# Attention with two expert layers: ACT's and DVE's copies out of the same PSUM banks modelled as taking turns, and the whole order made anew

## The chip, the cores and the metric

One core of a Trainium2 chip runs the program. The metric is the device time of one execution in microseconds (us). PE is the matrix engine, PEld its loading of weights, DVE the vector engine, ACT the scalar engine, POOL the GpSimd engine, SP the engine that issues the transfers.

## What is computed

Three stages follow each other: an attention in which a query sees only the keys whose 6 sign bits agree with its own, a layer with x·tanh(softplus(x)), and a layer with softmax times x and a layer norm. Inputs: q, k, v of 2 batches x 8 heads x 768 tokens x 64, `proj` 64 x 6, weights 512 x 2048 and back, 512 x 1024 and back (float64, read as pairs of 32-bit words).

```python
def _attn_ref(q, k, v, proj) -> np.ndarray:
...
    q_bits = (np.einsum('bhsd,dk->bhsk', q, proj) > 0).astype(np.int64)
    k_bits = (np.einsum('bhsd,dk->bhsk', k, proj) > 0).astype(np.int64)
...
    mask = q_bucket[:, :, :, None] == k_bucket[:, :, None, :]
    scores = scale * np.matmul(q, k.transpose(0, 1, 3, 2))
    scores = np.where(mask, scores, -1000000000.0)
...
    return np.matmul(attn, v).astype(np.float32)
...
def _moe_ref(x, w_in, w_out) -> np.ndarray:
    h = x @ w_in
    sp = np.where(h > 20.0, h, np.log1p(np.exp(np.minimum(h, 20.0))))
    g = h * np.tanh(sp)
    return (g @ w_out).astype(np.float32)
...
def _moe2_ref(x, w_in, w_out, g_ln) -> np.ndarray:
    h = x @ w_in
...
    solu = h * sm
...
    return (ln @ w_out).astype(np.float32)
```

## The kernel before, in words

**The stages.** The 16 heads are worked on in 8 pairs (0 to 7). Each head has 6 tiles of 128 queries by 768 keys, so there are 96 tiles. A tile's steps are `score` (PE, L1238), `max` (DVE, L1245) and `bias` (DVE, two one-column rows, L1249 and L1250), `exp` (ACT, L1254), a split of the result into two f16 halves and its transposition (by DMA for four tiles in six; for the two others by PE, L1273, ACT, L1277, and DVE, `tlo`, L1282), and `weigh`, the product with v (PE, L1305 to L1307). The first expert layer has 48 units, each of 12 products up, 11 element steps (`mi`) on ACT, DVE and POOL, and 12 products down. The second has 12 tiles. Weights come as 48 chunks (`w`): a load, a first step on ACT (L728), four on DVE (L730, L732, L734, L736), one on ACT and one on POOL or DVE. Eight chunks (0 to 7) are meant for the time of the attention, the others for that of the first layer.

**The preparation of a pair.** While the tiles of pair n-1 run, pair n is prepared. For each of its two heads and for q and k, PE makes 6 transposes into two PSUM banks (`turn`, L1163), and ACT copies the banks out into a tile A (`evac`, L1180, 128 partitions). For q a second copy of half of the same banks goes to a tile B on DVE (L1171, 64 partitions). There are 16 of these second copies, two for each pair. For k the rest of B comes by DMA (`copy`). PE then multiplies A with the projection (`bits`, L1204), DVE compares (`sign`, L1212), and small DMAs put the bits into B. Only then can the pair's scores start. `vmax` (DVE, L1091) and some one-column steps `vs` prepare v.

**What sets the order.** A scheduler in the program, class `Order`, sets the order of all instructions on all engines before they are issued. It knows a cost for each step (`COST`), a delay from engine to engine (`LATENCY`) and the rings and banks. Of the steps that could start within 0.1 us of the earliest it takes the one that is due first. A step's due time is its place in the work plus an offset of its kind from `PHASE`, some 130 numbers. Nothing moves at run time: each engine works its list from top to bottom, and where a step waits, all behind it on that engine wait too. In the scheduler's model before, the first and second copies of the same banks (`("evac", n, h, 0)` and `("evac", n, h, 2)`) are two readers that may run at the same time:

```python
op(("evac", n, h, o), A if e == "A" else V, COST["evac" + e], d, "evac" + f, [s], [("A%d" % o, n, h)])
if again and (o if n == 0 else not o):
    g = again[h]
    op(("evac", n, h, 2), A if g == "A" else V, COST["evac" + g], d, "evac" + f, [("st", n, h, 0)],
       [("B", n, h, 0)])
```

Of the kernel before, what the change touches and what calls it, by code (L numbers as in the profile page):

```python
# [32 lines left out]
    score=2.89, max=21.69, bias=-20.48, exp=-7.37, hi=37.60, lo=-74.88, tdma=47.79, tr0=9.51, thi0=14.05,  # L33
    tlo0=2.17, tr1=10.84, thi1=28.04, tlo1=16.57, weigh=17.46, norm0=29.45, norm1=6.67, norm2=-77.92,
    load=19.06, vload=18.96, split0=-188.88, rest0=28.62, split1=-216.02, rest1=37.27, turn=-44.19,
    evac=-204.06, copy=-27.06, bits0=-103.88, bits1=-136.11, sign=51.37, bdma=40.93, vmax=21.86, vs0=-271.50,
    vs1=9.08, vs2=-210.73, vs3=-129.45, vs4=-56.64, vs5=-127.12, vs6=-290.81, vs7=144.62, vs8=-328.13,
    vh=70.16, vl=45.25, first=63.48, turn_=6.48, evac_=195.41, copy_=-35.91, bits_=94.54, sign_=168.35,
    bdma_=-9.06, vload_=-304.47, vmax_=171.56, vs_=87.04, vh_=-22.87, vl_=-122.68, second=35.58, wload=28.78,
    w0=-41.17, w1=84.02, w2=-26.10, w3=26.15, w4=31.29, w5=19.05, w6=290.37, wpace=-25.50, wat=214.24,  # L40
    wlate=-420.19, turngap=-246.21, x0_=-6.98, x1_=-173.02, x2_=44.49, load_=10.81, const0=66.52,
    begin0=-146.26, vs8_=150.21, outlag=-5.17, up=-162.02, a0=-14.23, a1=40.52, a2=25.54, a3=14.48, a4=30.07,
    a5=-71.43, a6=11.38, a7=-135.40, a8=-17.97, a9=76.71, a10=229.81, da=51.52, db=-112.61, ky0=101.10,
    ky1=110.82, x0=37.16, x1=118.52, x2=72.93, sy0=21.03, sy1=8.66, u2=24.00, n0=-198.44, n1=78.28, n2=130.92,
    n3=-69.22, n4=-178.31, n5=-31.52, n6=140.09, n7=224.60, n8=-279.51, n9=-111.63, n10=-196.61, n11=-61.38,
    n12=-275.68, n13=3.09, t2=-8.41, l0=-92.90, l1=222.42, d2=202.96, ot=-141.26, od=-47.76, wloadL=-156.21,
    w0L=2.89, w1L=23.01, w2L=229.21, w3L=-26.73, w4L=229.00, w5L=-89.36, w6L=-69.41, begin1=-117.25,
    begin2=-102.32, begin3=76.98, const1=123.70, const3=67.06, load0_=-1.00,
)


# [25 lines left out]
class Order:  # L77
# [38 lines left out]
    def shared(self, o):  # L116
# [7 lines left out]
        if k in ("hi", "sy", "mg"):  # L124
            return True
# [12 lines left out]
    def run(self):  # L138
# [64 lines left out]
        for _ in range(n):  # L203
            best = None
            for e, line in queue.items():
                cand = []
                for r, i in line:
                    r = max(r, free[e])
                    if ops[i][7]:
                        r = ring(i, r)[0]  # L210
                        if r is None:
                            continue
# [1203 lines left out]
```

## Time and profile before

| what | us |
|---|---|
| three timed runs: median, lowest, highest | 654.56, 653.5, 655.46 |
| profiled execution, its own time | 653.04 |
| span of its trace, first to last instruction | 651.3 |

The profiled execution took 1.7 us more than its span, for what lies before the first and after the last instruction. In rows of the trace, times count from the span's start, a row gives start and duration in us, engine, line, operation, what is written and read, and in brackets how long the engine had been idle before it and what ended that.

### The profile page before, as it was taken

How to read it: one execution, taken by the hardware profiler on the slowest of the kernel's cores; microseconds unless marked ns; L12 is line 12 of the kernel's file. 1: busy time of each engine (PE TensorE's matmuls, PEld its weight loads, DVE VectorE, ACT ScalarE, POOL GpSimd, SP SyncE). 2: the span in 40 equal slices, each digit the busy share in tenths (PEclk: the TensorE clock that was granted, in tenths of full speed). 3: DMA queues.
4: the chain of work that ended last, by engine and by line, in shares of the span. 5: the costliest groups of instructions: out<-in, count | busy, mean ns of one | idle time of the engine just before them, and what ended most of it. 6: DMA issues, size and time to landing. Idle time of an engine off the chain costs nothing.

```text
span 651.3 us, 12308 instructions
## 1 busy us (share of the span) xinstructions
PE 622.2 (96%) x4460; PEld 513.1 (79%) x4460; DVE 558.7 (86%) x1149; ACT 444.0 (68%) x722; POOL 367.5 (56%) x301
## 2 busy tenths in 40 slices
PE   7889999999899899999999999999999999999997
PEld 6668787888778788878888777788788888788885
DVE  4899798898989999999999999999999776675652
ACT  5689897998999986766565566656566545565543
POOL 4678868777765675566666666455476421222210
PEclk9799899999999999999999999999999999999999
DMA  7979978989898892312333322212121022322221
GB/s 203 219 166 148 243 162 159 170 212 166 180 186 165 151 205 76 97 50 79 98 98 97 98 97 66 94 61 70 35 97 34 1 64 45 81 71 81 66 64 49
DMA packets 146909, 73.36 MB, mean 113 GB/s; under 512 B 125344, under 2 KB 139808, under 8 KB 146848
## 3 DMA queue, kind: packets, MB, share of 16 engines
q1 hardware_dynamic: 146848, 72.58, 47.5%
q8 instruction: 35, 0.57, 0.4%
q14 instruction: 26, 0.21, 0.1%
HBM read 34.68 MB, written 3.15 MB: 58 GB/s over the span
## 4 chain that ended last, share of the span: by engine, by line
PE 42%; DVE 22%; ACT 6%; issue 5%; DMA 1%; POOL 0%; DVEq 0%; ACTq 0%; SPq 0%
PE banks L835 4%; PE banks L837 3%; PE banks L940 3%; PE banks L836 3%; PE banks L944 3%; PE banks L941 3%; PE banks L896 3%; PE banks L891 3%; PE banks L892 3%; PE banks L1029 3%; PE banks L1027 3%; DVE mx L1245 3%; PE banks L1028 3%; DVE a L865 2%; DVE a L853 2%
## 5 line engine op out<-in xcount | busy, mean ns | idle before, releaser
L1287 POOL TENSOR_TENSOR store<-store 128x768 f16<-128x768 f32 x64 | 104.9, 1651 | 48.6 <-ACT store L1265 44.3
L1254 ACT ACTIVATE store<-banks,mx 128x768 f32<-128x768 f32 x96 | 92.4, 998 | 12.3 <-DVE mx L1250 5.0
L1245 DVE TENSOR_REDUCE mx<-banks 128x1 f32<-128x768 f32 x96 | 89.4, 946 | 3.1 <-PE banks L1238 2.0
L869 POOL TENSOR_TENSOR n<-c,a 128x512 f32<-128x512 f32 x48 | 63.8, 1329 | 44.6 <-DVE a L865 42.3
L877 POOL TENSOR_TENSOR gl<-n,gh 128x512 fp32r<-128x512 f32 x48 | 62.9, 1310 | 33.4 <-ACT gh L874 33.0
L835 PE MATMUL banks<-xh,w 128*128 128x512 f32 x192 | 76.6, 399 | 2.5 <-DVE a L865 1.6
L891 PE MATMUL banks<-gh,w 128*128 128x512 f32 x192 | 75.8, 395 | 0.9 <-ACT gh L874 0.8
L837 PE MATMUL banks<-xh,w 128*128 128x512 f32 x192 | 75.7, 394 | 0.0
L836 PE MATMUL banks<-xl,w 128*128 128x512 f32 x192 | 75.4, 393 | 0.0
L892 PE MATMUL banks<-gh,w 128*128 128x512 f32 x192 | 75.3, 392 | 0.0
L859 ACT ACTIVATE a<-n,two 128x512 f32<-128x512 f32 x48 | 34.8, 724 | 56.7 <-DVE n L855 56.4
L896 PE MATMUL banks<-gl,w 128*128 128x512 f32 x192 | 72.4, 394 | 0.0
L743 POOL TENSOR_TENSOR w<-wf,w 128x512 fp32r<-128x512 f32 x40 | 51.7, 1293 | 35.2 <-ACT w L741 33.9
L1238 PE MATMUL banks<-A,A 128*128 128x384 f32 x192 | 58.5, 387 | 8.4 <-ACT store L1254 7.4
L1305 PE MATMUL banks<-v,store 128*128 128x65 f16 x576 | 60.0, 193 | 2.3 <-DVE store L1282 1.9
L1306 PE MATMUL banks<-v,store 128*128 128x64 f16 x576 | 59.8, 194 | 0.0
L1307 PE MATMUL banks<-v,store 128*128 128x65 f16 x576 | 59.6, 192 | 0.0
L1305 PEld LDWEIGHTS <-store 128*128 128x128 f16 x576 | 53.0, 96 | 5.0 <-issue 4.6
L1306 PEld LDWEIGHTS <-store 128*128 128x128 f16 x576 | 53.3, 97 | 2.9 <-issue 2.5
L1265 ACT ACTIVATE store<-store 128x768 f16<-128x768 f32 x64 | 53.3, 849 | 0.2
L1307 PEld LDWEIGHTS <-store 128*128 128x128 f16 x576 | 53.5, 99 | 0.0
L1238 PE MATMUL banks<-B 76*128 76x384 f32 x192 | 51.5, 350 | 0.0
(131 smaller groups left out, 1731.7 us busy)
## 6 DMA issues: line engine op xcount, KB each, us to landing
wr<-in_moe_w_in_dram SPq DMA_DIRECT2D x24, 512.0 KB
wr<-in_moe_w_out_dram SPq DMA_DIRECT2D x24, 512.0 KB
vr<-in_v_dram SPq DMA_DIRECT2D x8, 384.0 KB
B<-A SPq DMA_DIRECT2D x16, 192.0 KB
out_dram<-ot SPq DMA_DIRECT2D x12, 256.0 KB
q<-in_q_dram SPq DMA_DIRECT2D x7, 384.0 KB
k<-in_k_dram SPq DMA_DIRECT2D x7, 384.0 KB
B<-bits SPq DMA_DIRECT2D x32, 36.0 KB
```

The costliest lines, as they stand in the source:

```text
L835: nc.tensor.matmul(h, lhsT=wh[:, ks], rhs=xh, start=(kk == 0), stop=False)
L836: nc.tensor.matmul(h, lhsT=wh[:, ks], rhs=xl, start=False, stop=False)
L837: nc.tensor.matmul(h, lhsT=wl[:, ks], rhs=xh, start=False, stop=(kk == KD - 1))
L891: nc.tensor.matmul(y, lhsT=wh[:, os], rhs=g_t[u][0], start=first, stop=False)
L892: nc.tensor.matmul(y, lhsT=wl[:, os], rhs=g_t[u][0], start=False, stop=False)
L1238: nc.tensor.matmul(s[:, half, 0:NH], lhsT=opnd[nm, p, j, 0][:, cc], rhs=opnd[nm, p, j, 1][:, hs], start=(i == 0), stop=(i == 1),)
L1245: nc.vector.reduce_max(m[:, 1:2], two_banks("s", t)[:, :, 0:NH], axis=AX.XY, negate=True)
L1254: nc.scalar.activation(kept("e", t).rearrange("p (a n) -> p a n", a=2), two_banks("s", t)[:, :, 0:NH], AF.Exp, bias=m[:, 3:4], scale=m[:, ...
L1287: nc.gpsimd.tensor_tensor(p16[:, 1], kept("e", t), p16[:, 0], op=ALU.subtract)
L1305: nc.tensor.matmul(o, lhsT=pt[:, 0, kc, :], rhs=vh, start=(kc == 0), stop=False)
L1306: nc.tensor.matmul(o[:, 0:D], lhsT=pt[:, 0, kc, :], rhs=vl, start=False, stop=False)
L1307: nc.tensor.matmul(o, lhsT=pt[:, 1, kc, :], rhs=vh, start=False, stop=(kc == NC - 1))
```

## The change

The scheduler gets a rule: of the ACT copy to A and the DVE copy to B of the same banks, whichever is put second becomes ready only when the first is done, plus the delay between the engines. All numbers of `PHASE` were set anew, and with them the order of all instructions on all engines is another one. The same instructions are issued, as many of each kind and size. Two more ways of making the second copy, from tile A, on ACT (`a`) or on DVE (`v`), are written into the code; `again` is still "VV", so they are not used.

```diff
 PHASE = dict(
-    score=2.89, max=21.69, bias=-20.48, exp=-7.37, hi=37.60, lo=-74.88, tdma=47.79, tr0=9.51, thi0=14.05,
+    score=3.38, max=19.53, bias=-65.87, exp=-8.79, hi=46.12, lo=-15.66, tdma=47.09, tr0=9.55, thi0=-33.26,
...
@@ -82,6 +83,7 @@
         self.spare = dict(e=2, p16=1)
+        self.other, self.port = {}, set()
...
@@ -210,6 +212,9 @@
                         if r is None:
                             continue
+                    k = self.other.get(i)
+                    if k is not None and done[k] is not None:
+                        r = max(r, done[k] + LATENCY[frm[k]].get(e, 0.0))
                     cand.append((r, due[i], i))
...
@@ -326,8 +331,13 @@
                     g = again[h]
-                    op(("evac", n, h, 2), A if g == "A" else V, COST["evac" + g], d, "evac" + f, [("st", n, h, 0)],
-                       [("B", n, h, 0)])
+                    op(("evac", n, h, 2), A if g in "Aa" else V, COST["evac" + g], d, "evac" + f,
+                       [("st", n, h, 0) if g in "AV" else ("A0", n, h)], [("B", n, h, 0)])
+                    if g == "v":
+                        order.port.add(("evac", n, h, 2))
+                if again and (o if n == 0 else not o) and g in "AV":
+                    a, b = (order.index["evac", n, h, i] for i in (0, 2))
+                    order.other[a], order.other[b] = b, a
```

Three places on DVE show how the order moves. In the changed program the lines of these functions stand 10 to 13 further down (the second copy is L1184 there, `max` L1258, `sign` L1225).

Before, on DVE, the preparation of pair 1, some 15 us into the span: the last one-column steps for v, both second copies (`B<-banks`), the compare of pair 0's second head (`bits<-banks,cs`), the first `max` and the first weight step (`banks<-wf`).

```order
L1119 TENSOR_SCALAR pw<-pw 128x1
L1171 TENSOR_SCALAR B<-banks 64x768 x2
L1212 TENSOR_SCALAR bits<-banks,cs 24x768
L1245 TENSOR_REDUCE mx_97<-banks 128x1
L730 TENSOR_SCALAR banks<-wf 128x512
L1249 TENSOR_SCALAR mx_97<-mx_97 128x1
L1250 TENSOR_SCALAR mx_97<-mx_97 128x1
```

The same place after the change:

```order
L1129 TENSOR_SCALAR pw<-pw 128x1
L740 TENSOR_SCALAR banks<-wf 128x512
L1184 TENSOR_SCALAR B<-banks 64x768 x2
L742 TENSOR_SCALAR banks<-banks 128x512
L1225 TENSOR_SCALAR bits<-banks,cs 24x768
L744 SCALAR_TENSOR_TENSOR banks<-wr,banks 128x512
L746 SCALAR_TENSOR_TENSOR wf<-wr,banks 128x512
L1258 TENSOR_REDUCE mx_97<-banks 128x1
```

The four DVE steps of weight chunk 0 have moved forward: the first stands ahead of the second copies, the other three ahead of the first `max`.

Before, on DVE, the changeover to pair 5, some 127 us into the span: the last `max` of pair 4, both second copies, then the first `max` of pair 5.

```order
L1245 TENSOR_REDUCE mx_104<-banks 128x1
L1249 TENSOR_SCALAR mx_104<-mx_104 128x1
L1250 TENSOR_SCALAR mx_104<-mx_104 128x1
L1171 TENSOR_SCALAR B<-banks 64x768 x2
L1245 TENSOR_REDUCE mx_97<-banks 128x1
L1282 SCALAR_TENSOR_TENSOR store<-banks,store 128x384
```

After the change, from the norm of an earlier head (`r`) to the second of the two copies and the step behind it:

```order
L1328 TENSOR_TENSOR r<-banks,pcol 128x6
L1330 RECIPROCAL r<-r 128x6
L1184 TENSOR_SCALAR B<-banks 64x768
L1118 TENSOR_SCALAR pw<-banks 128x1
L1332 SCALAR_TENSOR_TENSOR xn<-banks,pw,r 128x6x64
L1120 TENSOR_SCALAR pw<-pw 128x1
L744 SCALAR_TENSOR_TENSOR banks<-wr,banks 128x512
L1125 RECIPROCAL pw<-pw 128x1
L1127 TENSOR_SCALAR pw<-pw 128x1
L1295 SCALAR_TENSOR_TENSOR store<-banks,store 128x384
L746 SCALAR_TENSOR_TENSOR wf<-wr,banks 128x512
L1184 TENSOR_SCALAR B<-banks 64x768
```

Between the two second copies there now stand eight steps: four one-column steps for v (`pw`), the end of a head's norm (`xn`), two weight steps (L744, L746) and one `tlo` (`store<-banks,store`).

Before, on DVE, the changeover to pair 3, from its second copies (some 70 us into the span) to the compare (`bits<-banks,cs`) and what stands behind it:

```order
L1171 TENSOR_SCALAR B<-banks 64x768 x2
L1245 TENSOR_REDUCE mx_97<-banks 128x1
L1282 SCALAR_TENSOR_TENSOR store<-banks,store 128x384
L1249 TENSOR_SCALAR mx_97<-mx_97 128x1
L1250 TENSOR_SCALAR mx_97<-mx_97 128x1
L1282 SCALAR_TENSOR_TENSOR store<-banks,store 128x384
L1245 TENSOR_REDUCE mx_98<-banks 128x1
L1249 TENSOR_SCALAR mx_98<-mx_98 128x1
L1250 TENSOR_SCALAR mx_98<-mx_98 128x1
L1212 TENSOR_SCALAR bits<-banks,cs 48x768
L1091 TENSOR_REDUCE am<-vr 128x1
L1245 TENSOR_REDUCE mx_99<-banks 128x1
```

After the change:

```order
L1184 TENSOR_SCALAR B<-banks 64x768
L1295 SCALAR_TENSOR_TENSOR store<-banks,store 128x384
L1184 TENSOR_SCALAR B<-banks 64x768
L1258 TENSOR_REDUCE mx_97<-banks 128x1
L1258 TENSOR_REDUCE mx_98<-banks 128x1
L1262 TENSOR_SCALAR mx_97<-mx_97 128x1
L1263 TENSOR_SCALAR mx_97<-mx_97 128x1
L1262 TENSOR_SCALAR mx_98<-mx_98 128x1
L1263 TENSOR_SCALAR mx_98<-mx_98 128x1
L1295 SCALAR_TENSOR_TENSOR store<-banks,store 128x384
L1101 TENSOR_REDUCE am<-vr 128x1
L1225 TENSOR_SCALAR bits<-banks,cs 48x768
```

One `tlo` now stands between the copies, and `vmax` (`am<-vr`) stands ahead of the compare, no longer behind it.

## Rows read from the trace of the kernel before

**Rows 1.** Stretches: length; busy PE, PEld, DVE, ACT, POOL; clock, DMA share, GB/s

```profile
0.00:237.00 237.00, 215.09 (x2523) 183.86 (x2524) 206.16 (x522) 204.59 (x292) 169.75 (x131) 0.97 0.89 183
237.00:507.00 270.00, 266.97 (x1327) 214.99 (x1324) 262.88 (x432) 167.00 (x289) 163.78 (x126) 1.00 0.26 79
```

**Rows 2.** Groups of instructions: xcount | busy us, mean ns | idle before us <-releasers

```profile
L1171 DVE TENSOR_SCALAR B<-banks 64x768 fp32r<-64x768 f32 x16 | 15.1, 948 | 12.1 <-ACT A L1180 7.6 <-PE banks L1163 2.4 <-DMA B<-bits 2.1
L1180 ACT ACTIVATE A<-banks 128x768 fp32r<-128x768 f32 x32 | 25.6, 814 | 8.2 <-DVE B L1171 5.2 <-PE banks L1163 2.9
L1212 DVE TENSOR_SCALAR bits<-banks,cs 48x768 fp32r<-48x768 f32 (+1 forms) x9 | 9.6, 1063 | 3.8 <-PE banks L1204 2.4 <-ACT w L741 1.4
```

**Rows 3.** Timeline of ACT, the changeover to pair 3

```profile
72.79 0.81 ACT L1180 ACTIVATE A<-banks 128x768 fp32r<-128x768 f32 x1 [0.16 <-DVE B L1171]
```

**Rows 4.** Timeline of DVE, second copies and compares with a wait

```profile
15.29 1.81 DVE L1171 TENSOR_SCALAR B<-banks 64x768 fp32r<-64x768 f32 x2 [2.27 <-ACT A L1180]
...
50.54 1.07 DVE L1212 TENSOR_SCALAR bits<-banks,cs 48x768 fp32r<-48x768 f32 x1 [1.42 <-ACT w L741]
...
71.80 0.95 DVE L1171 TENSOR_SCALAR B<-banks 64x768 fp32r<-64x768 f32 x1 [0.72 <-PE banks L1163]
...
78.01 1.07 DVE L1212 TENSOR_SCALAR bits<-banks,cs 48x768 fp32r<-48x768 f32 x1 [1.13 <-PE banks L1204]
...
127.83 0.95 DVE L1171 TENSOR_SCALAR B<-banks 64x768 fp32r<-64x768 f32 x1 [0.79 <-PE banks L1163]
...
153.28 0.95 DVE L1171 TENSOR_SCALAR B<-banks 64x768 fp32r<-64x768 f32 x1 [1.39 <-ACT A L1180]
...
184.69 0.95 DVE L1171 TENSOR_SCALAR B<-banks 64x768 fp32r<-64x768 f32 x1 [0.57 <-ACT A L1180]
...
188.73 1.07 DVE L1212 TENSOR_SCALAR bits<-banks,cs 48x768 fp32r<-48x768 f32 x1 [0.53 <-PE banks L1204]
```

**Rows 5.** Groups: the DVE steps that the change moves into those places

```profile
L1245 DVE TENSOR_REDUCE mx<-banks 128x1 f32<-128x768 f32 x96 | 89.4, 946 | 3.1 <-PE banks L1238 2.0 <-ACT A L1180 0.9
L1282 DVE SCALAR_TENSOR_TENSOR store<-banks,store 128x384 f16<-128x384 f32 x64 | 35.0, 550 | 2.7 <-ACT store L1277 2.1
L730 DVE TENSOR_SCALAR banks<-wf 128x512 f32<-128x512 f32 x48 | 33.0, 688 | 0.7 <-ACT wf L728 0.4 <-ACT store L1254 0.2
L1091 DVE TENSOR_REDUCE am<-vr 128x1 f32<-128x768 f32 x8 | 7.5, 943 | 1.1 <-DMA vr<-in_v_dram 1.1
```

**Rows 6.** Timelines of ACT and PE at the start

```profile
26.36 0.67 ACT L728 ACTIVATE wf<-wr 128x512 f32<-128x512 f32 x1 [0.48 <-DMA wr<-in_moe_w_out_dram]
28.33 1.01 PE L1238 MATMUL banks<-A,A 128*128 128x384 f32 x2 [2.27 <-ACT store L1254]
```

**Rows 7.** Timeline of PE in the first expert layer

```profile
371.21 0.50 PE L891 MATMUL banks<-gh,w 128*128 128x512 f32 x1 [0.82 <-ACT gh L874]
383.41 0.50 PE L835 MATMUL banks<-xh,w 128*128 128x512 f32 x1 [0.43 <-DVE wf L736]
```

**Rows 8.** Chain that ended last, from 180 to 190 us, by line

```profile
by line: ACT A L1180 20.4%; ACT store L1254 20.2%; DVE B L1171 19.1%; DVE mx L1245 17.3%; PE banks L1238 9.6%; PE banks L1163 7.2%; DVE store L1282 4.7%; issue 3.1%; DVE mx L1250 1.3%; DVE mx L1249 0.6%; ACTq L1254 0.4%
```

**Rows 9.** Timeline of ACT, first weight steps that waited for their load

```profile
13.88 0.68 ACT L728 ACTIVATE wf<-wr 128x512 f32<-128x512 f32 x1 [2.06 <-DMA wr<-in_moe_w_in_dram]
...
173.71 0.66 ACT L728 ACTIVATE wf<-wr 128x512 f32<-128x512 f32 x1 [1.10 <-DMA wr<-in_moe_w_in_dram]
...
196.99 0.67 ACT L728 ACTIVATE wf<-wr 128x512 f32<-128x512 f32 x1 [1.18 <-DMA wr<-in_moe_w_in_dram]
```

**Rows 10.** Stretches, columns as in rows 1; clock 1.00 is 2.4 GHz

```profile
28.00:34.40 6.40, 6.07 (x26) 5.66 (x27) 4.34 (x11) 5.02 (x7) 4.29 (x5) 0.50 0.30 64
...
72.00:75.40 3.40, 3.40 (x11) 3.03 (x12) 2.52 (x6) 3.24 (x6) 3.32 (x4) 0.52 0.92 204
...
122.00:130.00 8.00, 7.71 (x98) 6.60 (x98) 6.28 (x12) 7.45 (x12) 5.61 (x5) 1.00 1.20 169
```

**Rows 11.** Timeline of PE, the transposes of the changeover to pair 3

```profile
68.53 2.27 PE L1163 MATMUL banks<-identr,sp 128*128 128x128 f32 x18 [0.85 <-ACT store L1254]
```

More of the change, by code (lines that the diff above doesn't have):

```diff
@@ L32 @@
 PHASE = dict(
-    score=2.89, max=21.69, bias=-20.48, exp=-7.37, hi=37.60, lo=-74.88, tdma=47.79, tr0=9.51, thi0=14.05,
[L34 to L47, printed above, removed]
@@ L48 @@
-    begin2=-102.32, begin3=76.98, const1=123.70, const3=67.06, load0_=-1.00,
+    score=3.38, max=19.53, bias=-65.87, exp=-8.79, hi=46.12, lo=-15.66, tdma=47.09, tr0=9.55, thi0=-33.26,
+    tlo0=-62.01, tr1=11.04, thi1=9.03, tlo1=13.12, weigh=17.51, norm0=26.43, norm1=-69.47, norm2=-60.41,
+    load=7.63, vload=26.19, split0=-209.02, rest0=-14.46, split1=-114.89, rest1=-2.88, turn=-158.91,
+    evac=-361.95, copy=-350.38, bits0=-444.55, bits1=-228.32, sign=153.12, bdma=-171.64, vmax=108.26,
+    vs0=-308.92, vs1=-371.38, vs2=-393.59, vs3=-145.17, vs4=-438.80, vs5=-13.61, vs6=-597.77, vs7=150.18,
@@ new lines @@
+    vs8=-570.75, vh=54.46, vl=-45.05, first=-198.82, turn_=103.45, evac_=238.54, copy_=-161.87, bits_=401.21,
+    sign_=442.43, bdma_=-228.13, vload_=-345.05, vmax_=357.96, vs_=136.89, vh_=33.52, vl_=-437.02,
+    second=9.07, wload=320.29, w0=16.38, w1=289.47, w2=-67.86, w3=93.26, w4=48.79, w5=-0.94, w6=366.69,
+    wpace=-28.80, wat=187.14, wlate=-600.69, turngap=-310.22, x0_=-5.24, x1_=-111.87, x2_=84.49, load_=-69.26,
+    const0=72.86, begin0=-37.06, vs8_=427.52, outlag=-17.49, up=-208.23, a0=-41.64, a1=36.42, a2=14.13,
@@ new lines @@
+    a3=-127.83, a4=27.89, a5=-284.31, a6=-148.77, a7=-275.37, a8=161.81, a9=116.21, a10=268.20, da=86.24,
+    db=-139.94, ky0=298.36, ky1=-25.70, x0=180.33, x1=143.21, x2=11.70, sy0=297.52, sy1=156.27, u2=-155.47,
+    n0=-331.94, n1=-136.70, n2=261.70, n3=85.09, n4=200.24, n5=144.50, n6=312.75, n7=538.09, n8=-303.05,
+    n9=-102.14, n10=-219.32, n11=-529.01, n12=-105.86, n13=88.41, t2=406.26, l0=-579.38, l1=168.49, d2=600.51,
+    ot=-280.00, od=338.37, wloadL=-160.93, w0L=67.85, w1L=41.93, w2L=358.04, w3L=-2.18, w4L=64.57,
@@ L49 @@
+    w5L=-187.51, w6L=-57.01, begin1=-356.07, begin2=-43.37, begin3=79.81, const1=291.20, const3=59.53,
+    load0_=34.29,
 )
@@ L54 @@
     weigh=0.555, norm0=0.075, norm1=0.106, norm2=0.531, split=0.8, rest=1.79, turn=0.515,
-    evacA=0.691, evacV=0.865, warm=3.2, bits=0.7, sign=0.985, vmax=0.87, vs0=0.11, vs1=0.2, vs2=0.11,
+    evacA=0.691, evacV=0.865, evaca=0.733, evacv=0.469, warm=3.2, bits=0.7, sign=0.985, vmax=0.87, vs0=0.11, vs1=0.2, vs2=0.11,
     vs=0.07, vs8=0.884, vh=0.733, firstA=0.413, firstD=0.469, w0=0.56, w1=0.602, w2=0.602,
@@ L123, in shared @@
         k = key[0]
-        if k in ("hi", "sy", "mg"):
+        if k in ("hi", "sy", "mg") or key in self.port:
             return True
@@ L1167, in qk_again @@
         src = two_banks("st", p, h, 0)[0:64, :, 0:NH]
-        if again[h] == "A":
+        if again[h] in "av":
+            src = opnd["A", p, h, 0][0:64].bitcast(F32).rearrange("p (a n) -> p a n", a=2)
+            (nc.scalar.copy if again[h] == "a" else nc.vector.tensor_copy)(dst, src)
+        elif again[h] == "A":
             nc.scalar.activation(dst, src, AF.Copy, scale=SC)
```

## The prediction

> **What bounds the kernel now.** I read the stretches first, since the change touches all three stages but in the attention alone adds a rule. In the 270 us of the first expert layer PE is busy for 266.97 us and DVE for 262.88 us: there no order can gain more than a few us. In the first 237 us, the attention, no engine is full: PE 215.09, DVE 206.16, ACT 204.59 us [rows 1]. That leaves PE 21.9, DVE 30.8 and ACT 32.4 us of idle time, and what is to be gained lies there.
>
> Next come the groups of instructions. The 16 second copies on DVE have 12.1 us of idle time ahead of them, more than any other DVE group of the attention, 7.6 us of it put down to ACT's copies; ACT in turn stands 5.2 us ahead of its copies until a second copy on DVE ends [rows 2]. So the two do take turns on the chip already, in both directions: at 72.79 us ACT starts a copy just after DVE's, which ran from 71.80 for 0.95 us [rows 3, 4]. The 12.8 us are what the old model did not know of. The turns themselves remain after the change. What can change is whether the waiting engine has other work in its list at that point.
>
> Then the timeline of DVE gives single places [rows 4], and the chain tells whether such a place sets the time: from 180 to 190 us, the changeover to pair 7, ACT's copies hold 20.4% of the chain, DVE's 19.1%, the transposes 7.2% [rows 8]. The alternation itself is on the path there, and that speaks for caution: work that fills a wait does not shorten the alternation. It is worth something only because that work need not be done later.
>
> **The change, part by part.** Work and sizes are the same, so I count four things: waits that get covered on DVE, work that comes forward, the first layer, and what stays.
>
> 1. *Waits ahead of the second copies.* Each credit is the wait or the work newly put into it, whichever is less.
>    - Pair 1: 2.27 us at 15.29 [rows 4]. A weight step of 0.69 us [rows 5] moves ahead of the copies. It needs ACT's step of 13.88 us, which takes 0.68 us [rows 9], so it runs from about 14.7 to 15.4 and delays the copy by 0.1: credit 0.6.
>    - Pair 3: 0.72 us at 71.80 [rows 4]; a `tlo` of 0.55 us [rows 5] now stands between the copies: 0.55.
>    - Pair 5: 0.79 us at 127.83 [rows 4]; eight steps now stand between the copies, the two weight steps alone over 1.3 us: 0.79.
>    - Pair 6: 1.39 us at 153.28, ahead of its first copy [rows 4]; two weight steps, 1.38 us, stand there in place of a `tlo` of 0.55 [rows 5]: 0.83.
>    - Pair 7: 0.57 us at 184.69 [rows 4]; two `tlo` and two weight steps between the copies, where one of each was: 0.57.
>    - Pairs 0, 2 and 4 get nothing like it: 0.
>    Sum 3.34 us.
> 2. *Waits ahead of the compares.* Pair 2 waits 1.42 us at 50.54 [rows 4]; one more `max` of 0.95 us [rows 5] comes before it: 0.95. Pair 3 waits 1.13 us at 78.01 [rows 4]; `vmax`, 0.94 us [rows 5], now precedes it: 0.94. Pair 7 waits 0.53 us at 188.73 [rows 4]; norms and four weight steps of chunk 5 come between: 0.53. Sum 2.42 us.
> 3. *Work that comes forward.* Chunks 3 to 7 are converted earlier and more evenly. Before the last `max`, DVE now also does the four steps of chunk 7, 4 x 0.69 = 2.75 us, and leaves two `tlo`, 1.10 us, for later [rows 5]. I charge 1.65 us. The first layer could give it back, since DVE is nearly full there; PE is fuller [rows 1], so I count nothing back.
> 4. *First layer.* PE waits 0.82 us at 371.21 and 0.43 us at 383.41 [rows 7]. There three chunks (28 to 30) are finished on DVE within one unit; the new order finishes one in each unit. Credit 1.25 us.
> 5. *The start.* PE's longest wait, 2.27 us at 28.33, is behind an exponential that stands in ACT's list behind a weight step whose load lands at 26.36 [rows 6]. In the new order that step still stands ahead of the same exponential, and the loads ahead of it in SP's list carry the same bytes: 0. In the second layer the order is nearly the old one and PE sets the pace: 0.
>
> Sum: -3.34 - 2.42 + 1.65 - 1.25 = -5.36 us. Against the profiled execution's own 653.04 us that is 647.7. That execution lies 1.5 us below the median of the three runs shown; I set the forecast against the median: 654.56 - 5.36 = **649.2 us**.
>
> Bounds. Nothing may be won by the covers and all of the charge stay: -1.25 + 1.65, so +0.4 us. At the other end all idle time before second copies and compares goes, 12.1 + 3.8 us [rows 2], and the charge with it: -17. I stand a third of the way, since a cover on one engine leaves the alternation itself on the path [rows 8].
>
> **The rivals.**
>
> *No change (within 0.3%).* The alternation is the path at the changeovers, as at pair 7 [rows 8], and DVE, filled there, has no lack of time afterwards, with 30.8 us idle in the attention [rows 1]. Then the covers are worth nothing and the work that comes forward costs nothing either; the first layer's 1.25 us remain: 653.3. For it: no engine is full in the attention. Against it: long runs of `max` end each other's waits between changeovers.
>
> *Slower.* Each engine works in list order, and a weight chunk's first step on ACT blocks all exponentials behind it until its load has landed. Such steps waited 2.06, 1.10 and 1.18 us [rows 9]. Chunks 3 to 7 are now needed 8 to 14 tiles earlier, in a stretch whose transfers are busier. If each of the five waits the longest of these, 10.3 us, against the 2.28 us that the two late ones cost now, ACT loses 8.0 us; less the 5.36 us, that is +2.7: 657.2. It decides once these added waits exceed 5.36 us. For it: the DMA share is 0.89 over the attention [rows 1]. Against it: the loads have moved up in SP's list too.
>
> *Faster still, by the clock.* From 72.00 to 75.40 us PE ran at a granted clock of 0.52, so at 1.2 GHz; before that it had waited 0.85 us and then done 24 transposes (a row of 18 and one of 6) with nothing else between [rows 10, 11]. At the changeover to pair 5, with products with v between the same 24 transposes, the clock stayed at 1.00 [rows 10]. The new order has such products between the transposes of pair 3 as well. If the clock holds, 3.4 us at half speed become 1.7; if the stretch from 28.00 to 34.40 at 0.50 [rows 10] goes too, another 3.2. Together -4.9: 644.3. The Trainium skill's page "TensorE: Matmul & The Clock Gate", section "HAM oscillation — how this bites in real kernels", says that a PE that has to pause between groups of products falls back to the lower clock each time, and that the work should be ordered so that it need not pause; by it the first half of this rival would hold, and the trace agrees at 72.00 us, where the wait of 0.85 us came before. Against the second half: at the start the new order puts all four groups of transposes of pair 1 in one row, and the wait that comes before it is pinned by a load.
>
> **How the numbers follow.** A measurement of this kernel tells about 0.3%, 2.0 us, from no change: faster is below 652.6, slower above 656.5. The forecast gets 0.40, the clock 0.16, no change 0.29, slower 0.15. Faster is 0.40 + 0.16 = 0.56. The range reaches from 645.0, near the clock's 644.3, to 657.0, near the slower rival's 657.2; half of each of these two cases lies outside, with a rest of the others that is about 2 in 10. The forecast alone would be 646.3 to 652.1, its covers of 5.76 us half as large again or half as large.
>
> **What would show it.** Right: the idle time before the 16 second copies falls from 12.1 to about 8.8 us, that before the compares from 3.8 to about 1.5; DVE's idle time in the attention falls by 5.8 us and the last exponential comes some 4 us earlier; PE has no two waits of 0.4 us or more near unit 23 in the first layer. Wrong: the idle time of these groups falls but turns up before `max` or `exp` (no change), or ACT's waits for weight loads in the attention rise past 9 us (slower), or stretches at 0.50 are gone (clock). If the last exponential comes as late as before and the time still falls, my place, the attention, was wrong.

## The result, and the profile after the change

The changed kernel took **650.31 us** (median of 7, 648.44 to 651.58) against 655.29 us beside it (median of 7): ratio 0.9915, 95% interval 0.9887 to 0.9942, so 5.0 us less. A second measurement, on another occasion, gave 653.37 us against 655.13, ratio 0.997 (0.9936 to 1.0004), 1.8 us less; alone it is not clear of no change. Why the two differ is told under "The clock". The profiled execution of the changed kernel took 651.06 us, its span is 649.2 us; the profiled execution before took 653.04. So these two traces differ by 2.0 us only, and the trace of the second measurement spans 651.3 us, as long as before's. The rows below are of the first trace of the changed kernel.

First the groups that answer to [rows 2] (columns as there; lines stand 10 to 13 further down):

```profile
L1258 DVE TENSOR_REDUCE mx<-banks 128x1 f32<-128x768 f32 x96 | 89.6, 947 | 4.8 <-PE banks L1251 4.7
L1184 DVE TENSOR_SCALAR B<-banks 64x768 fp32r<-64x768 f32 x16 | 15.1, 946 | 2.6 <-ACT A L1193 1.9 <-PE banks L1173 0.4
L1225 DVE TENSOR_SCALAR bits<-banks,cs 48x768 fp32r<-48x768 f32 (+1 forms) x9 | 9.6, 1064 | 4.8 <-PE banks L1217 3.6 <-ACT store L1267 1.2
L1112 DVE TENSOR_REDUCE am<-banks 1x1 f32<-1x128 f32 x8 | 2.2, 272 | 3.2 <-PE banks L1109 3.2
L1193 ACT ACTIVATE A<-banks 128x768 fp32r<-128x768 f32 x32 | 25.6, 822 | 3.4 <-PE banks L1173 3.4
```

The idle time ahead of the 16 second copies has fallen from 12.1 to 2.6 us, and ACT no longer waits for DVE's copies at all (5.2 us before). But the idle time ahead of the compares (L1225) rose from 3.8 to 4.8 us (two waits of it below, at the changeovers to pairs 5 and 6), that ahead of the maxima (L1258) from 3.1 to 4.8, and a step for v (L1112) now waits 3.2 us, where it waited 0.5.

```profile
131.65 1.07 DVE L1225 TENSOR_SCALAR bits<-banks,cs 48x768 fp32r<-48x768 f32 x1 [1.35 <-PE banks L1217]
...
160.20 1.07 DVE L1225 TENSOR_SCALAR bits<-banks,cs 48x768 fp32r<-48x768 f32 x1 [1.73 <-PE banks L1217]
```

How much of it is left in sum shows where DVE's time is counted up to the same event, the first expert unit's first DVE step (233.77 us before, 230.99 after) and the last unit's (507.45 and 503.47). Stretches of before, then of after, columns as in [rows 1]:

```profile
0.00:233.77 233.77, 211.86 (x2476) 181.15 (x2477) 202.93 (x517) 201.36 (x287) 167.69 (x130) 0.97 0.88 182
0.00:507.45 507.45, 482.51 (x3845) 399.22 (x3846) 469.49 (x953) 372.04 (x580) 333.98 (x258) 0.99 0.55 128
```

```profile
0.00:230.99 230.99, 209.62 (x2469) 180.09 (x2470) 203.25 (x516) 201.18 (x287) 169.81 (x132) 0.97 0.90 184
0.00:503.47 503.47, 478.22 (x3833) 396.73 (x3834) 467.74 (x949) 370.51 (x577) 333.99 (x257) 0.99 0.56 129
```

DVE's idle time in the attention is 233.77 - 202.93 = 30.8 us before and 230.99 - 203.25 = 27.7 after, 3.1 us less; up to the last unit it is 38.0 and 35.7, 2.2 us less. That is near the difference of the spans, 651.3 - 649.2 = 2.1. Of the 9.5 us taken away ahead of the second copies two thirds turned up before other DVE steps. In the second trace nearly all of it did: the copies wait 2.0 us there, but DVE's idle time in the attention is 233.60 - 203.44 = 30.2 us.

Two single rows of DVE before and two after show the first expert layer's unit 23 and unit 24 (the first step of each):

```profile
367.45 0.68 DVE L853 TENSOR_SCALAR a<-banks 128x512 f32<-128x512 f32 x1
378.21 0.68 DVE L853 TENSOR_SCALAR a<-banks 128x512 f32<-128x512 f32 x1
```

```profile
369.94 0.69 DVE L863 TENSOR_SCALAR a<-banks 128x512 f32<-128x512 f32 x1
376.28 0.68 DVE L863 TENSOR_SCALAR a<-banks 128x512 f32<-128x512 f32 x1
```

The step from unit 23 to unit 24 sank from 10.8 to 6.3 us. But unit 23 itself comes 2.5 us later than before, although the attention ended earlier: the last exponential starts at 230.87 us, before it did at 234.45. So 6.1 us were lost between the last exponential and unit 23. In the second trace the last exponential starts at 233.48 us, only 1.0 us earlier than before, and unit 23 at 371.97 us, so 5.5 us were lost. From the last exponential to the first step of unit 24 it takes 143.8 us before and 145.4 and 144.8 after: the shorter step from unit 23 to unit 24 does not make up for what is lost ahead of it. ACT's rows in that stretch (first trace), the last exponential and the two first weight steps with the longest waits:

```profile
230.87 0.99 ACT L1267 ACTIVATE store<-banks,mx 128x768 f32<-128x768 f32 x1
...
239.75 0.68 ACT L738 ACTIVATE wf<-wr 128x512 f32<-128x512 f32 x1 [2.71 <-DMA wr<-in_moe_w_out_dram]
...
245.94 0.67 ACT L738 ACTIVATE wf<-wr 128x512 f32<-128x512 f32 x1 [2.34 <-DMA wr<-in_moe_w_in_dram]
```

From 230 to 250 us DVE was busy for 19.79 of 20 us before, and now for 17.72 (stretches of before and after):

```profile
230.00:250.00 20.00, 20.00 (x278) 17.21 (x279) 19.79 (x40) 15.46 (x27) 13.95 (x11) 1.00 0.77 173
230.00:250.00 20.00, 19.29 (x279) 16.93 (x278) 17.72 (x34) 13.91 (x25) 10.05 (x9) 1.00 0.75 154
```

### The profile page after: what moved, and what is told of

It is laid out like the page before. It is cut to its first block, busy times and chain, and to the rows that moved or that the text cites. A ratio compares the mean times of both kernels' runs of the same rounds, so it can differ in the third digit from the quotient of the medians.

```text
span 649.2 us, 12285 instructions
## 1 busy us (share of the span) xinstructions
PE 620.0 (96%) x4460; PEld 512.9 (79%) x4460; DVE 560.0 (86%) x1149; ACT 444.2 (68%) x722; POOL 369.9 (57%) x301
## 4 chain that ended last, share of the span: by engine, by line
PE 60%; DVE 18%; ACT 8%; DMA 6%; issue 4%; POOL 3%; SPq 1%; DVEq 0%; ACTq 0%; POOLq 0%
PE banks L906 5%; PE banks L901 5%; PE banks L902 5%; PE banks L845 5%; PE banks L846 5%; PE banks L847 4%; PE banks L1251 4%; DVE mx L1258 4%; DMA store<-store 3%; PE banks L1039 3%; PE banks L1037 3%; PE banks L951 3%; PE banks L954 3%; PE banks L950 3%; PE banks L1038 3%
## 5 line engine op out<-in xcount | busy, mean ns | idle before, releaser
L1258 DVE TENSOR_REDUCE mx<-banks 128x1 f32<-128x768 f32 x96 | 89.6, 947 | 4.8 <-PE banks L1251 4.7
```

Of the source, the lines that this page charges most:

```text
L1258: nc.vector.reduce_max(m[:, 1:2], two_banks("s", t)[:, :, 0:NH], axis=AX.XY, negate=True)
```

## The clock

The clock of [rows 10] in the changed kernel, at the start and at the changeover to pair 3:

```profile
18.00:25.00 7.00, 6.20 (x24) 4.38 (x23) 4.55 (x8) 4.39 (x6) 6.21 (x5) 0.52 1.04 325
32.00:39.00 7.00, 6.58 (x29) 5.76 (x27) 5.52 (x14) 5.53 (x9) 3.41 (x3) 0.54 0.31 64
72.00:75.40 3.40, 3.40 (x62) 3.40 (x59) 2.35 (x4) 3.40 (x6) 3.12 (x3) 1.00 1.03 240
```

The stretch near 72 us now holds 2.4 GHz. The start has two stretches near 1.2 GHz, as before, where one ran from about 18 to 21 us and the other is that of [rows 10]; the first has become twice as long. Over the first 45 us the mean clock is 0.89 before and 0.85 after. Stretches of before:

```profile
18.00:20.00 2.00, 1.86 (x6) 1.62 (x7) 2.00 (x6) 1.79 (x3) 0.35 (x1) 0.50 1.01 312
20.00:22.00 2.00, 2.00 (x11) 1.33 (x10) 1.55 (x3) 1.59 (x2) 2.00 (x2) 0.77 0.98 316
0.00:45.00 45.00, 36.09 (x228) 29.39 (x229) 33.09 (x85) 31.24 (x44) 26.91 (x37) 0.89 0.78 188
```

The same kernel, run again, had a third one, from 208 to 212 us. Such stretches come in some executions and not in others, and each execution lists the mean clock of its span. Some executions of the second measurement, clock and us:

```
after:  0.977 657.2, 657.4   0.979 655.1, 655.5   0.984 652.9   0.989 649.3, 649.7, 650.1
before: 0.977 661.0          0.979 656.8 to 659.5  0.986 655.1   0.990 653.5 to 657.3   0.994 652.3, 652.4, 652.4
```

A straight line through each kernel's executions falls by 5.6 us (after, 12 executions) and 3.6 us (before, 32) for each 0.01 of clock. At 0.985 the lines give 652.3 +- 0.6 and 656.7 +- 0.5. **At the same clock the new order is thus 4.4 us faster.** The two lines are not parallel: at 0.979 they lie 3.2 us apart, at 0.989 5.2. A comparison at equal clock also leaves out what an order does to the clock itself; whether the new order makes low clocks likelier is not shown. In the second measurement the changed kernel ran at a lower clock than before (mean 0.983 and 0.989), which took back some 2 to 3 us; in the first its mean was 0.988. This explains most of the difference between 5.0 and 1.8 us.

## The experiments

Times are medians; "line" is the value of the straight line at a clock of 0.985, with twice its standard error.

| kernel | us | beside it, before | ratio, 95% | line | line of before |
|---|---|---|---|---|---|
| changed, second time | 653.37 | 655.13 | 0.997 (0.9936 to 1.0004) | 652.3 +- 0.6 | 656.7 |
| new attention, old layers | 652.12 | 654.59 | 0.9978 (0.9943 to 1.0012) | 653.6 +- 0.5 | 655.9 |
| old attention, new layers | 659.34 | 654.59 | 1.0062 (1.0037 to 1.0087) | 660.6 +- 0.9 | 655.9 |
| the rule, old numbers | 674.57 | 654.59 | 1.0283 (1.0245 to 1.0321) | 673.4 +- 1.9 | 655.9 |
| second copy from tile A | 658.06 | 654.59 | 1.006 (1.0035 to 1.0085) | 655.8 +- 1.0 | 655.9 |
| covers undone | 655.72 | 655.13 | 1.001 (0.9979 to 1.0042) | 655.8 +- 0.5 | 656.7 |
| bunch restored | 662.71 | 655.13 | 1.0096 (1.0063 to 1.0129) | 658.6 +- 1.9 | 656.7 |
| start and seam mended | 656.49 | 655.13 | 1.0008 (0.9979 to 1.0036) | 654.0 +- 0.6 | 656.7 |
| before, bunch spread | 659.7 | 654.65 | 1.0052 (1.0021 to 1.0084) | 659.4 +- 1.1 | 656.4 |
| one hold of the clock | 650.16 | 654.65 | 0.993 (0.9904 to 0.9956) | 652.4 +- 0.8 | 656.4 |
| two holds | 652.15 | 654.65 | 0.9949 (0.9918 to 0.998) | 653.8 +- 1.1 | 656.4 |
| clock held at the start | **646.22** | 655.15 | **0.9871 (0.983 to 0.9912)** | | |

### The halves of the table

The changed kernel with the offsets of the two expert layers put back, and the kernel before with the new ones:

```diff
-    outlag=-17.49, up=-208.23, a0=-41.64, a1=36.42, a2=14.13,
+    outlag=-5.17, up=-162.02, a0=-14.23, a1=40.52, a2=25.54,
...
```

> The changed kernel with the offsets of the first and second expert layer set back to the old ones (up, a0 to a10, da, db, ky, x0 to x2, sy, u2, n, t2, l, d2, ot, od, the late weight steps, outlag); the attention's order is the new one up to its last tiles. Theory (the gain is made in the attention): the last exponential starts some 3.7 us earlier than in the kernel before, 229 to 231 us, and the whole is 3 to 6 us faster than before; the three weight chunks in unit 23 are back and cost about 5 us at that unit. Rival (the layers' order brings the gain): the whole within 1.5 us of before.

> The kernel before with the new offsets of the two expert layers alone; the attention's order is the old one. Theory: the last exponential starts where it did, 234 to 235 us, idle time ahead of the second copies stays near 12 us, and the whole is within 2 us of before. Rival (the layers): 4 to 6 us faster than before, with the long unit 23 gone.

By the lines the new attention alone brings 2.3 us and the new layers alone cost 4.7, together +2.4; the whole change brings 4.4. Neither theory of the two runs came true: the gain is not made by the attention alone, and the new layers alone are a loss. Nearly 7 us belong to neither half, but to their fit. Single traces show where: from the last exponential to the first step of unit 24 it takes 143.8 us before, 146.8 with the new attention alone, 148.7 with the new layers alone, and 145.4 and 144.8 in the changed kernel's two traces. So each half alone loses 3.0 and 4.9 us in that stretch, and both together 1.0 to 1.6. The trace of the new layers alone has a stretch at a clock of 0.50 in there (278 to 284 us), so its figure is too high by up to half of that stretch. In the trace of the new attention alone the covers are kept (2.0 us idle before the second copies) and the step from unit 23 to 24 is back at 10.6 us; its last exponential starts at 235.47 us, not at the 229 to 231 expected, in an execution at a clock of 0.979.

### The rule alone

The changed kernel with all old offsets:

```diff
-    score=3.38, max=19.53, bias=-65.87, exp=-8.79, hi=46.12, lo=-15.66,
+    score=2.89, max=21.69, bias=-20.48, exp=-7.37, hi=37.60, lo=-74.88,
...
```

> The scheduler's new rule with all the old offsets. Theory (a scheduler that knows of the turns fills them by itself): idle time ahead of the second copies on DVE falls from 12.1 us to under 6 us, ACT's wait for them from 5.2 us to under 2 us, and the whole is 0 to 4 us faster than before though nothing was tuned for it. Rival (the offsets bring it, the rule does not): idle time ahead of the copies stays above 9 us, the whole as before or up to 5 us slower.

Its groups (second copies, ACT's first weight steps):

```profile
L1183 DVE TENSOR_SCALAR B<-banks 64x768 fp32r<-64x768 f32 x16 | 15.0, 944 | 3.3 <-PE banks L1172 1.6 <-ACT A L1192 0.9 <-ACT store L1277 0.5
```

```profile
L737 ACT ACTIVATE wf<-wr 128x512 f32<-128x512 f32 x48 | 32.2, 670 | 26.5 <-DMA wr<-in_moe_w_in_dram 18.3 <-DMA wr<-in_moe_w_out_dram 5.9 <-POOL gl L886 1.7
```

The rule by itself covers the waits at the copies (12.1 to 3.3 us), and yet the kernel is 2.8% slower, more than either theory allowed. The old offsets, fed with other ready times, place the weight steps badly: 26.5 us idle ahead of ACT's first steps, 16.7 in the kernel before, 14.6 in the changed kernel. That this is the whole loss is not shown. The rule describes the turns that the traces show; the gain needs the offsets. The new offsets without the rule were not run.

### The second copy from tile A

The way `v`, which the change writes into the code without using it:

```diff
-    again="VV",
+    again="vv",
```

> The changed kernel with the second copy made from tile A in SBUF instead of the PSUM banks, so that no bank is read by two engines and ACT never waits for DVE; the scheduler makes its order anew with the same offsets. Theory (the turns were most of what could be gained at the copies, and the new order already covers them): idle time ahead of the second copies stays under 4 us, the copy itself is shorter than its 0.95 us, and the whole is within 3 us of the changed kernel either way. Rival (the turns still cost the changed kernel several us): 4 us or more faster than the changed kernel.

```profile
L1180 DVE CAST B<-A 64x768 fp32r<-64x768 f32 x16 | 15.3, 962 | 8.4 <-ACT A L1193 8.1
```

No bank is shared any more, and ACT's copies wait for none of DVE's. But the copy takes 962 ns, no less than out of the banks (946), while the scheduler's cost for it is 469 ns; and it cannot start before ACT's copy has ended: 8.1 of the 8.4 us of idle time ahead of it end with that. The kernel is slower than before by its median and equal by its line, which lies 3.5 us above the changed kernel's. Since the order was made with a cost of half the true one, the run does not tell what a second copy from tile A could give with an order made for it.

### The covers undone

The changed kernel, its order altered by a list of moves after the scheduler's run (two of 15 shown):

```diff
     keys = order.run()
+    moves = [(('tlo', 19, 1), ('evac', 3, 0, 2)),
...
+             (('w', 4, 1), ('evac', 6, 0, 2)),
...
+    for x, y in moves:
+        keys.remove(x)
+        keys.insert(keys.index(y) + 1, x)
```

> The changed kernel, with the steps that stand ahead of or between the second copies of pairs 1, 3, 5, 6 and 7 put behind them on DVE where the data allow it (of pair 5's eight steps two stay); all else in the same order. Theory A, the forecast's first term (a covered wait is time won, since the covering work need not be done later): DVE's idle time ahead of the second copies rises from 2.6 us by some 2 to 4 us, and the time by as much, to about 653. Theory B (ACT's and DVE's alternation is the path at the changeovers, and DVE catches up afterwards): the idle time rises by as much, the time stays within 1 us of the changed kernel's 650.3.

Groups of this kernel, then of the changed kernel's second run, which ran beside it:

```profile
L1258 DVE TENSOR_REDUCE mx<-banks 128x1 f32<-128x768 f32 x96 | 89.5, 948 | 3.3 <-PE banks L1251 3.1
L1184 DVE TENSOR_SCALAR B<-banks 64x768 fp32r<-64x768 f32 x16 | 15.1, 948 | 8.7 <-ACT A L1193 5.5 <-PE banks L1173 2.9
L1225 DVE TENSOR_SCALAR bits<-banks,cs 48x768 fp32r<-48x768 f32 (+1 forms) x9 | 9.6, 1064 | 2.8 <-PE banks L1217 1.6 <-ACT store L1267 1.2
```

```profile
L1258 DVE TENSOR_REDUCE mx<-banks 128x1 f32<-128x768 f32 x96 | 89.6, 948 | 4.6 <-PE banks L1251 4.4
L1184 DVE TENSOR_SCALAR B<-banks 64x768 fp32r<-64x768 f32 x16 | 15.0, 945 | 2.0 <-ACT A L1193 1.4 <-PE banks L1173 0.4
L1225 DVE TENSOR_SCALAR bits<-banks,cs 48x768 fp32r<-48x768 f32 (+1 forms) x9 | 9.6, 1064 | 4.4 <-PE banks L1217 3.2 <-ACT store L1267 1.2
```

The copies wait 6.7 us more, and the compares and maxima 1.6 and 1.3 less: without the work between them the copies end sooner, and what comes next is ready sooner. What is left, 3.8 us, is near what the time rose by: 2.4 us by the medians, 3.5 (655.8 - 652.3) by the lines. **Here a cover was worth about half of the wait it filled.** With the covers 3.5 of the 4.4 us at equal clock go; the waits are from one trace of each kernel.

### The bunch of weight chunks

The changed kernel with the DVE steps of chunks 29 and 30 put back into unit 23 (two of 23 moves), and the kernel before with those of chunks 27 to 30 drawn apart (two of 43):

```diff
+    moves = [(('w', 29, 1), ('mi', 23, 2)),
+             (('w', 29, 2), ('mi', 23, 3)),
...
```

```diff
...
+             (('w', 28, 3), ('mi', 22, 5)),
+             (('w', 28, 4), ('w', 28, 3)),
...
```

> The changed kernel, with the DVE steps of weight chunks 29 and 30, and what hangs on them, put back into unit 23 and the start of unit 24 of the first expert layer, as before. Theory A, the forecast's fourth term (PE's waits there are time won): PE waits near unit 23 come back and the time rises by 1.25 us or more, up to the 4.4 us by which the step from unit 23 to unit 24 differs between the two profiles. Theory C (DVE, idle for only some 4 us in the whole layer in either kernel, sets its pace, and a bunch on it only moves work from one unit to another): the step from unit 23 to 24 grows by 4 us, the units before it come earlier by as much, and the time stays within 1 us.

> The kernel before, with nothing but the steps of weight chunks 27 to 30 moved: on DVE they stand one to five steps further ahead, so that a unit of the first expert layer finishes about one chunk, as after the change, and no longer three in unit 23; ACT's and POOL's steps of these chunks move with them. Theory A (the forecast's fourth term: PE's waits at that place are time won): faster than before by 1.25 us, up to some 4 us, as far as the step from unit 23 to unit 24, 10.8 us before and 6.3 after, sinks without the units ahead of it growing. Theory C (DVE sets the pace of the layer and the bunch only shifts work): the step sinks, units 21 to 23 grow by as much, within 1 us of before at the same granted clock.

Both are slower than what they started from, the first by 9.3 us by the medians (6.3 by the lines), the second by 5.0 (3.0). Timelines, PE in the first, then ACT and PE in the second:

```profile
383.16 0.50 PE L845 MATMUL banks<-xh,w 128*128 128x512 f32 x1 [1.99 <-ACT w L751]
387.73 0.80 PE L847 MATMUL banks<-xh,w 128*128 128x512 f32 x1 [3.65 <-POOL w L753]
```

```profile
366.59 0.66 ACT L728 ACTIVATE wf<-wr 128x512 f32<-128x512 f32 x1 [2.73 <-DMA wr<-in_moe_w_in_dram]
...
367.83 0.50 PE L891 MATMUL banks<-gh,w 128*128 128x512 f32 x1 [3.03 <-ACT gh L874]
```

In the first, chunks 29 and 30 come too late for unit 25, and PE waits 5.6 us in two places: a heavier bunch than before's, whose waits were 0.82 and 0.43 us [rows 7]. In the second, ACT's first step of chunk 28 stands ahead of an element step and waits for its load, and PE waits 3.03 us behind it. The step from unit 23 to unit 24, which this run was to shorten, is still 10.3 us. So neither gives the price of before's bunch. In both traces the clock is at 0.50 in a stretch near these waits (383.5 to 393.8 us in the first, 368.8 to 372.2 in the second), so part of the loss is the clock's. They show that PE's waits of 2 to 3.7 us in this layer reach the end of the program, which speaks against the view that a bunch only shifts DVE's work; how much of the 4.4 us from 10.8 to 6.3 was a gain stays open.

### Start and seam mended

The two places where the changed kernel's trace shows new waits (three of 12 moves):

```diff
...
+             (('bits', 1, (0, 1), 0), ('score', 3)),
...
+             (('w', 9, 0), ('thi', 94, 1)),
...
+             (('w', 10, 0), ('w', 9, 5)),
...
```

> The changed kernel with two stalls mended by hand. At the start pair 1's twelve products with the projection, which stand between the first and the second score and hold ACT for 2.83 us, go behind the fourth score, and DVE's maxima of tiles 0 and 1 go ahead of the steps for v. At the seam ACT's first steps of chunks 9 and 10, which wait 2.71 and 2.34 us for their loads, go behind steps that are ready. Theory D (these two places are where the changed kernel gives back what it gains): faster than the changed kernel by 2 to 4 us, 646 to 648; the second exponential comes 2 to 3 us earlier and ACT's waits for weight loads near 240 us go. Theory E (at the start ACT and DVE have slack that the next 30 tiles use up; at the seam DVE lacks work that is ready, whatever ACT does): within 1 us of 650.3, and the 36th exponential comes at the same time as in the changed kernel.

> The changed kernel once more, for a second profile: by either theory 650.3 us within 1.5, with the milestones (36th exponential, last exponential, unit 23, unit 24) within 1 us of those of its first profile. If they differ by more, differences of that size between two kernels' profiles say nothing.

The waits went: ACT's first steps of chunks 9 and 10 start without one, the second exponential comes at 25.59 us instead of 28.01. The time did not follow. This kernel is 3.1 us slower than the changed kernel beside it (1.7 by the lines). A stretch of its start:

```profile
16.00:32.00 16.00, 12.66 (x47) 9.83 (x48) 10.64 (x25) 10.15 (x13) 13.26 (x11) 0.57 1.04 283
```

PE ran near 1.2 GHz from 18 to 31 us in one piece. Over the first 45 us the mean clock is 0.85, as in the changed kernel, so the moves did not lengthen the time at 1.2 GHz, they changed where it lies. The fifth exponential comes at 35.18 us (32.63 in the second run of the changed kernel), and DVE's maxima wait 9.7 us in all (4.6 there). Which of the two, the place of the slow clock or the new order of the first scores, took back the gain is not shown. As for the second run of the changed kernel: its 36th exponential starts at 94.89 us, in the first run at 95.90, its last ones at 231.77 and 233.48 where the first run's last starts at 230.87. So single milestones of one kernel move by 1 to 3 us, and a smaller difference between two traces says nothing.

### The clock held

What the mended start left open is whether the half clock at the start reaches the end. Products without use go into PE's waits, into bank columns that nobody reads. With one hold and with two:

```diff
     def qk_turn(p, h, s):
...
+        for _ in range(9 if (p, h, s) == (1, 1, 1) else 0):
+            nc.tensor.matmul(banks[:, 6, 0:192], lhsT=ph[:, 0:128], rhs=ph, start=True, stop=True)
```

```diff
+        n = {(1, 1, 1): (9, 0), (2, 1, 1): (0, 1), (2, 1, 0): (0, 1)}.get((p, h, s), (0, 0))
...
             nc.tensor.transpose(dst.bitcast(F32R), src.bitcast(F32R), identr)
+            for _ in range(n[1]):
+                nc.tensor.matmul(mp[:, c // 3, 384:512], lhsT=ph[:, 0:128], rhs=ph[:, 0:128], start=True, stop=True)
```

> The changed kernel with 9 products without use (192 columns each, into a bank that nobody reads) put into PE's wait of 1.5 to 2 us ahead of pair 1's second 12 transposes, near 15 us. PE's clock was at 0.50 from about 18 to 24 us in every profile of the changed kernel. Theory F (the wait makes the clock fall, and the start is on the path): the clock stays at 1.00 until about 31 us, products that took 0.32 us take 0.17, and the time falls by some 2 to 3 us. Theory E (the start has slack that the next 30 tiles use up): the clock stays, exponentials 1 to 12 come earlier, the 36th comes as in the changed kernel, and the time stays within 1 us at the same granted clock elsewhere.

> As the run with one hold, and 12 more products without use (128 columns each, into unused columns of the same banks) one behind each of pair 2's transposes near 31 us, after which the clock fell a second time, from about 31 to 39 us. They lengthen these transposes by about 1 us at full clock. Theory F: the second stretch at 0.50 goes too, and the time falls by another 2 to 3 us, less the 1 us. Theory E: as with one hold, no gain or up to 1 us lost. If neither stretch goes, what makes the clock fall is not the empty time ahead of the transposes, and the clock's price stays unmeasured.

And with products in four waits of the start and behind each of pair 2's first 12 transposes:

```diff
             nc.tensor.transpose(dst.bitcast(F32R), src.bitcast(F32R), identr)
+            if p == 2 and h == 1:
+                nc.tensor.matmul(mp[:, c // 3, 384:512], lhsT=ph[:, 0:128], rhs=ph[:, 0:128], start=True, stop=True)
...
+        hold = {("bits", 0, (0,), 0): (6, 6, 0), ("vs", 0, 2): (6, 6, 0), ("turn", 1, 1, 1): (14, 6, 0), ("score", 4): (5, 2, 384)}
         for key in keys:
+            n, b, at = hold.get(key, (0, 0, 0))
+            for _ in range(n):
+                nc.tensor.matmul(banks[:, b, at:at + 128], lhsT=ph[:, 0:128], rhs=ph[:, 0:128], start=True, stop=True)
             do[key[0]](*key[1:])
```

> The changed kernel with products without use (128 columns each, into bank columns that nobody reads) in PE's waits of the first 30 us: 6 ahead of pair 0's first product with the projection, 6 ahead of a step for v, 14 ahead of pair 1's second 12 transposes, 5 ahead of the fifth score, and one behind each of pair 2's first 12 transposes. Theory F (empty time ahead of transposes makes the clock fall, and what PE loses there reaches the end): no stretch at 0.50 in the first 45 us in most executions, a mean clock of 0.995 or more, and the time 2 to 4 us under the changed kernel's 650.3, so 646 to 648; the best two runs of the kernel with two holds, at a clock of 0.999 and 1.000, took 647.2 and 645.5. Theory G (the falls come from something that such products don't change): the clock lies as in the changed kernel, 0.983 to 0.989, and the time at 650 to 653.

The first 45 us of the changed kernel's second run, with one hold, with two, and with the start held:

```profile
0.00:45.00 45.00, 36.88 (x221) 29.70 (x222) 32.70 (x83) 29.77 (x44) 24.97 (x35) 0.85 0.76 199
```

```profile
0.00:45.00 45.00, 37.33 (x254) 30.28 (x254) 33.52 (x86) 30.92 (x45) 25.97 (x35) 0.89 0.83 202
```

```profile
0.00:45.00 45.00, 38.93 (x205) 32.35 (x206) 30.87 (x79) 28.93 (x42) 23.53 (x34) 0.81 0.69 190
```

```profile
0.00:45.00 45.00, 39.54 (x317) 33.41 (x318) 35.24 (x88) 33.06 (x48) 28.08 (x38) 1.00 0.86 212
```

One hold shortened the first stretch at half clock (0.89 over the 45 us), two did not in the profiled execution (0.81, though its two best executions, at a clock of 0.999 and 1.000, took 647.2 and 645.5 us). With these waits of the start filled, the clock stays at 1.00. DVE gets 2.5 us more done in the 45 us than in the changed kernel (35.24 and 32.70), the last exponential starts at 226.50 us, and five of the six executions ran at 0.995 to 0.997. **646.22 us: this is faster than both kernels**, by 8.9 us than before. Part of that is the order, part the clock: before's own five executions at 0.994 and 0.995 in the second measurement took 652.3 to 654.2 us, where this kernel's four at 0.997 took 645.6 to 646.5 and its one at 0.995 took 649.4. The changed kernel without these products was not timed beside it, and the kernel before was not run with them, so what they would give the old order is open.

## Why the prediction was right

The forecast, 649.2 us, stands 1.1 us below the measured 650.31, the -5.36 us of the sum beside -5.0. The second measurement, 653.37 us, lies within the range too, but on the side of 652.6 that the forecast called no change. That the sum came so near the first is in part luck: two of its terms had the wrong sign, and the chance of the clock moves the median of one kernel by 3 us. The points below are read from single traces, whose spans lie 2.1 and 0.0 us under before's, less than the medians do, so they do not add up to the 5.0 us:

- **Waits ahead of the second copies** (-3.34 us). The waits went further than forecast, 12.1 to 2.6 us and not to 8.8, and ACT's 5.2 us went too. The step that the prediction leaned on, that a cover leaves the alternation on the path, held: with the covers undone 6.7 us of waits came back for 2.4 to 3.5 us of time. So the term was right in size by luck: a wait of twice the size, at half the worth.
- **Waits ahead of the compares** (-2.42 us). This step failed. Their idle time rose from 3.8 to 4.8 us: of the three waits that it named two are gone and that of pair 2 is still 1.20 us, and new ones of 1.35 and 1.73 us came at pairs 5 and 6, where it had looked for none. The covers undone show why: it falls to 2.8 us there. What is filled at the copies comes back in part at the compare behind them. I had counted the two as separate credits.
- **Work that comes forward** (+1.65 us). With the covers it was to bring the last exponential some 4 us earlier; it came 3.6 us earlier in one trace and 1.0 in the other, so the place held and the size is open. A further price fell behind it, where DVE had no chunk 7 left to do and was idle for 2.3 us between 230 and 250 us. That this hole is the price of the work done early is argued from the trace; no run shows it.
- **First layer** (-1.25 us). PE shows no wait of 0.4 us or more near unit 23, as forecast, and the step there shrank by 4.4 us. But the prediction counted nothing for the units ahead of it, and 5.5 to 6.1 us were lost there: from the last exponential to unit 24 the changed kernel takes 1.0 to 1.6 us more than before, not 1.25 less. The two runs on the bunch show only what lateness costs, not what its going was worth.
- **The start** (0). Wrong in principle: the start is on the path, as the held clock shows. The change made it a little slower: the clock over the first 45 us fell from 0.89 to 0.85. In the profiled executions that took as much time at 1.2 GHz as the stretch near 72 us gave back, and the mean clock of both is nearly the same, 0.990 and 0.989.
- **The rivals.** "Slower" needed more than 9 us of ACT's waits for loads in the attention; there were 1.3, and 3.1 in the second trace. Two such waits came where I had not looked, 2.71 and 2.34 us behind the last exponential, and mending them, together with the start, gained nothing. "Faster still": its first half came true (72 to 75.4 us at 1.00), its second did not, but was had in the last run by filling PE's waits. The page "TensorE: Matmul & The Clock Gate" of the Trainium skill, section "HAM oscillation — how this bites in real kernels", asks for work ordered so that PE need not pause between groups. The last run, which fills the pauses and does not remove them, fits that: 0.85 to 1.00 over the first 45 us. The pauses in the page's example are waits for loads and longer; here they were 0.5 to 2.0 us, and most of them ended with another engine's step.

What would have made the sum miss is the clock: 0.005 of it, the difference of the changed kernel's mean between the two measurements, is worth 2.8 us by its line, more than the compares' whole term.

## What to carry to other kernels

Count a covered wait at less than its length (here about half), and follow what the cover delays: here the next compare. Teach a scheduler the turns that a trace shows, then set its offsets again as a whole; the rule alone cost 2.8%, and the new layers' half of the table alone 0.6%. When one wait is counted as gone, count also what the steps around it lose: 4.4 us were won at unit 23, and 5.5 to 6.1 lost between the last exponential and it. Before explaining a difference of half a per cent, compare executions at the same granted clock, and look at the clock in the first stretch: filling PE's short waits there with products without use gave a median 4.1 and 7.2 us under the two of the changed kernel, taken on other occasions.

## What was not expected of the hardware

- Executions of one and the same kernel differ in their mean clock, from 0.977 to 0.989, and with it by 8 us; a stretch at half clock (0.57 from 208 to 212 us) stands in one profile of a kernel and not in the other.
- The clock fell behind short waits of PE. In the first trace of the changed kernel the stretch from 18 us on came behind a wait of 1.50 us ahead of transposes, the one from 32 us on behind waits of 0.66 and 0.46 us ahead of scores (rows of PE below). One wait filled was not enough: with two holds, the profiled execution fell at another of the waits, from 12 us on.
- A copy of 64x768 from a tile in SBUF took DVE 962 ns, one out of the banks 946.

```profile
16.99 1.67 PE L1173 MATMUL banks<-identr,sp 128*128 128x128 f32 x12 [1.50 <-POOL sp L1152]
...
29.05 0.62 PE L1251 MATMUL banks<-A,A 128*128 128x384 f32 x2 [0.66 <-ACT store L1267]
...
30.49 0.62 PE L1251 MATMUL banks<-A,A 128*128 128x384 f32 x2 [0.46 <-ACT store L1267]
```
